# Another order for the first heads of an attention, mixture-of-experts and feed-forward kernel

## The chip, the cores and the metric

The kernel runs on one core of a Trainium2 chip. The metric is the device time of one execution in microseconds. A core has TensorE (PE: matrix products, results to PSUM), VectorE (DVE), ScalarE (ACT), GpSimd (POOL) and SyncE (SP, which here only issues DMA transfers). Each engine works through its own list of instructions in order; a semaphore holds an instruction back until what it needs is there. So the order in which the program is written is the order of each engine's list.

## What is computed

```python
q_bits = (q @ proj) > 0;  k_bits = (k @ proj) > 0        # 6 bits per row: a hash bucket
mask   = q_bucket[:, :, :, None] == k_bucket[:, :, None, :]
scores = where(mask, q @ k.T / sqrt(D), -1e9)            # batch 2, 8 heads, seq 768, D 64
attn   = softmax(scores);  x = attn @ v                  # 16 heads in all
x = moe(x)          # 1536 tokens, width 512: argmax of 8 experts, relu(x w1) w2 times the gate
return moe2(x)      # 512 -> 2048 with a leaky relu -> 512
```

## The kernel before

Attention fills the first 240 us of the execution, and the two feed-forward stages the rest. Products are made in pairs of numbers (a rounded part A and a remainder B), so that the result keeps float32 accuracy.

**One head.** q and k of a head are loaded to a raw tile (`load`), rounded on ScalarE to A, and the remainder B made on GpSimd (`half0`; for head 0 on VectorE). A head's operand tile `op` (`OP[h%5]`, five of them) holds A and B in the places that the products need; the copies are made by ScalarE (`direct`, heads 0 to 2) or by DMA (`OD`, three transfers of A and two of B, for the others all of them). Rows 64 to 75 of two parts of `op` hold the hash bits, one-hot with a large weight: `Z0` (heads 0 and 1) or `Z` makes them in two halves of 384 columns, by three products (`misc<-A,pwh` and so on) and a threshold on VectorE, written into `op` directly by `Z0` and by two more DMA transfers (`op<-big`) by `Z`. Row 96 holds minus the maximum of each query. `clear` zeroes these rows beforehand on GpSimd. `one` and `idle(n)` are n filler products whose result nobody reads.

**The maxima.** Head h has six units u = 6h..6h+5, one for each 128 queries. `MAX(u, a)` makes the masked hash scores against half a of the keys (a product of 384 columns, `mxp`, 0.18 us apart), and VectorE takes the maximum of the half (`mx`). `POSTa` joins the halves (`mt`). For head 0 `mrow(half)` turns three of its columns over (three transposes on TensorE) and VectorE writes the row into `op`. For the others `POSTb` transposes once, VectorE makes `mr`, and one DMA transfer (`op<-mr`) brings it to row 96.

**The scores.** Step s = 6h+j takes 128 keys of head h: `ST(s, 0)` and `ST(s, 1)` are two products each (`st`) and the exponential on ScalarE (`E`), which needs the row of maxima. `EL(s)` makes a float16 rounding `Eh` on ScalarE and the remainder `El` on GpSimd. `AV(s)` multiplies them with the values, 18 products of 64 or 65 columns; it runs four steps behind (`LAG`), for two steps at once at every odd step. v is scaled to float16 first: `vam` (largest absolute value, VectorE, one instruction per head of a group of four), `vscale`, `vscale2` (a chain of six small VectorE instructions to `dg`, and one product), `vsplit` and `vtot`.

**What sets the order.** A loop over steps s writes for each step, in the order of the string `ORDER`, the halves of ST, the halves of MAX, EL, AV, and then what lists tied to the step hold; transfers are collected and issued at `D` of the next step. The table `PLAN` says at which step each of these is written: `Z2`, `Z3` (hash bits of heads 2 and 3), `v0`, `T`, `first` (the router) and others. How far the maxima run ahead is set by `LA` (units below s+6+LA+1 may be written at step s) and, for the first steps, by `cap` (units per step, otherwise two). Two PSUM buffers serve `misc`, five serve `mxp` and `st`. Before the loop the first three steps' first halves are written by hand, among fillers.

Of the kernel before, what the change touches and what calls it, by code (L numbers as in the profile page):

```python
# [11 lines left out]
F16 = mybir.dt.float16  # L12
# [13 lines left out]
LA = 4  # L26
# [14 lines left out]
    v0=(1, 3, 4), T3=(2, 2), Z3=(4, 5), T=(2, 4, 5, 7), Z=(8, 10), ld=0, am1=(4, 6, 8, 9), am=(4, 6, 8,  # L41
    10), sc=(13, 15), tot=3, tot0=6, sp=(-2, 4, 10, 18), cap=(3, 2, 0, 1), x=(1, 2, 7, 3), x3=(0, 1, 2, 2), x4=(9, 10, 13, 11), w1=(91, 92, 95, 96, 97, 98, 99, 100), ga=(87, 88, 90), vl=1, am0=(0, 0), Z2=(0, 1), x6=(0, 1, 6, 4), first=(57, 58, 59, 60, 66, 72, 75, 78, 83, 84, 85, 86),
# [461 lines left out]
def _program(base, tc, nc, q, k, v, proj, mod, w_gate, mbias, w1, w2, win, wout, alpha, out):  # L504
# [203 lines left out]
    clear(1)  # L708
    def half0(h):
        A[h]=ep.tile([128,768],F32R,tag="A",name="A",bufs=2); B[h]=ep.tile([128,768],F32R,tag="B",name="B",bufs=2)  # L710
        nc.scalar.activation(A[h],raw[h],AF.Copy)
        nc.gpsimd.tensor_tensor(out=B[h],in0=raw[h],in1=f32(A[h]),op=ALU.subtract)
    onesh=cp.tile([128,128],F16,tag="onesh",name="onesh")
    VT=cp.tile([33,4,65],F16,tag="vt",name="vt")
    FL=[cp.tile([33,768],F16,tag=f"fl{i}",name=f"fl{i}") for i in range(3)]
# [3 lines left out]
    def fill():  # L719
        for t in DG: nc.gpsimd.memset(t,0.0)  # L720
        nc.gpsimd.memset(onesh,2.0**-8)
        nc.gpsimd.memset(VT[:,:,64:65],0.0)
        nc.gpsimd.memset(VT[0:1,:,64:65],3.0)
        for t in FL: nc.gpsimd.memset(t,0.0)
        for t in VH: nc.gpsimd.memset(t[:,:,:,64:65],1.0)
        clear(3)
        clear(4)
# [87 lines left out]
    def Z0(h,half):  # L815
        p=misc()
        sl=slice(half*384,half*384+384)
        mm(p[0:44,0:384],p0h,A[h][:,sl],start=True,stop=False)
        mm(p[0:44,0:384],p0h,B[h][:,sl],start=False,stop=False)
        mm(p[0:44,0:384],p0l,A[h][:,sl],start=False,stop=True)  # L820
        for o_ in range(2):
            ps=slice(32*o_,32*o_+12)
            nc.vector.tensor_scalar(out=OP[h][64:76,1+o_,sl],in0=p[ps,0:384],scalar1=tv0[ps,0:1],scalar2=tv0[ps,1:2],op0=ALU.is_gt,op1=ALU.mult)
    mx={};flT={}
# [6 lines left out]
    def POSTa(h,c0=0,c1=6):  # L831
        nc.vector.tensor_reduce(out=mts[h%2][:,c0:c1],in_=mx[h][:,c0:c1],axis=AX.X,op=ALU.max)
# [78 lines left out]
    clear(2); half0(2)  # L911
    fill()
    for u in range(3):
        for a in range(2): MAX(u,a)
    POSTa(0,0,3); idle(7); mrow(0)
    for u in range(3,6):
        for a in range(2): MAX(u,a)
    POSTa(0,3,6)
    ahead=(0,1,2)
    Z0(1,0); ST(0,0)  # L920
    idle(2); mrow(1); idle(3); Z0(1,1); ST(1,0)
    for i in range(2): vam(0,slice(i,i+1))
    ST(2,0); idle(5)
    direct(2); OD(1,(3,4)); load(3); OD(2,(1,3,4)); vload(1)
    at(0,lambda:(load(4),load(5))); sl_at(0,flags0)
    for i in range(2): at(PLAN["am0"][i],lambda i=i:vam(0,slice(i+2,i+3)))
# [23 lines left out]
    for s in range(96+LAG+2):  # L950
        us=[u for u in range(nu,min(96,s+6+LA+1,nu+(PLAN["cap"][s] if s<len(PLAN["cap"]) else 2)))]; nu+=len(us)
        fs=dq[:]; dq.clear()
        for o in "aVDNbmnefopAL" if s==0 else ORDER:
# [3 lines left out]
            if o in "ab" and s<96 and not (o=="a" and s in ahead): ST(s,"ab".index(o))  # L957
            if o in "mn":
                for u in us: MAX(u,"mn".index(o))
            if o=="e" and 0<=s-1<96: EL(s-1)  # L960
# [607 lines left out]
```

## Time and profile before

| | |
|---|---|
| median of 3 runs | 687.61 us (685.89 to 688.62) |
| the profiled execution | 686.88 us, of which the span of the trace 685.1 us |
| TensorE busy | 656.4 us (96% of the span), mean granted clock 0.987 |
| VectorE, ScalarE, GpSimd busy | 446.7, 315.3, 236.0 us |

The span is the time from the first to the last instruction. The granted clock is a share of TensorE's full 2.4 GHz: 1.00 or, where it is held back, 0.50 (1.2 GHz); a figure between is a mean over a window. "Idle before" is how long an engine stood still ahead of an instruction, with what released it. Line numbers are those of the kernel before; in the changed kernel the same calls stand one or two lines earlier from `vam` on.

### The profile page before, as it was taken

Reading aid. Unit: us, or ns where it says so; the run is one execution under the profiler, and the core shown is the slowest. Engines: PE = TensorE matmul, PEld = TensorE weight load, DVE = VectorE, ACT = ScalarE, POOL = GpSimd, SP = SyncE. Lnnn points to the kernel's source line nnn. Section 1 sums busy time; section 2 is a strip of 40 time slices with the busy share of each in tenths; the row PEclk is TensorE's granted clock in tenths of the full one; section 3 lists DMA queues with packets and bytes.
Section 4 is the critical chain, followed back from the end, with each engine's and each line's share of the span. In section 5 each row is a group of like instructions: output and inputs, shape, how many; then the busy total and the mean of one; then the engine's idle time right before and its main releaser. Section 6 shows DMA issues by size and latency. Waiting matters only on the chain.

```text
span 685.1 us, 12778 instructions
## 1 busy us (share of the span) xinstructions
PE 656.4 (96%) x4938; PEld 556.2 (81%) x4938; DVE 446.7 (65%) x927; ACT 315.3 (46%) x536; POOL 236.0 (34%) x211
## 2 busy tenths in 40 slices
PE   7789999999999988999999999999999999999995
PEld 6578898998788878898888987888888888888884
DVE  6887878788888778455735668999443444433332
ACT  5567788887787843033423256665211111111111
POOL 8767999987967501310000202040030000200002
PEclk9979999999999999999999999999999999999998
DMA  8466864866603139385320834441020000100001
GB/s 217 129 146 142 187 154 97 185 185 138 140 11 125 49 107 395 119 321 201 108 61 11 285 120 154 131 146 62 1 93 1 15 16 0 47 16 0 1 0 61
DMA packets 32859, 75.02 MB, mean 110 GB/s; under 512 B 7276, under 2 KB 7366, under 8 KB 32534
## 3 DMA queue, kind: packets, MB, share of 16 engines
q1 hardware_dynamic: 29700, 64.43, 33.0%
q0 software_dynamic: 2960, 9.70, 4.3%
q8 instruction: 39, 0.64, 0.4%
q14 instruction: 30, 0.25, 0.1%
q10 hardware_dynamic: 130, 0.00, 0.0%
HBM read 49.79 MB, written 14.68 MB: 94 GB/s over the span
## 4 chain that ended last, share of the span: by engine, by line
PE 54%; DVE 1%; ACT 1%; issue 1%; POOL 1%; ACTq 0%; POOLq 0%
PE o L1413 19%; PE h L1387 18%; PE y L1074 8%; PE g L1054 8%; PE tr L1257 1%; POOL out_dram L1430 1%; PE tr L1041 0%; DVE w L1232 0%; DVE op L1232 0%; ACT op L1230 0%; DVE gl L620 0%; ACT gf L1391 0%; ACT q L1392 0%; ACT w L1230 0%; DVE big L1197 0%
## 5 line engine op out<-in xcount | busy, mean ns | idle before, releaser
L868 POOL TENSOR_TENSOR El<-E,Eh 128x768 f16<-128x768 f32 x87 | 142.7, 1652 | 36.6 <-ACT Eh L867 22.7
L863 ACT ACTIVATE E<-st 128x384 f32<-128x384 f32 x192 | 89.2, 494 | 53.3 <-PE st L862 49.8
L830 DVE TENSOR_REDUCE mx<-mxp 128x1 f32<-128x384 f32 x192 | 97.6, 548 | 9.2 <-PE mxp L829 8.7
L617 ACT ACTIVATE gh<-gf 128x512 fp32r<-128x512 f32 x48 | 30.3, 631 | 142.7 <-PE o L1413 132.2
L867 ACT ACTIVATE Eh<-E 128x768 f16<-128x768 f32 x94 | 79.8, 849 | 0.0
L861 PE MATMUL st<-op 97*128 97x384 f32 x192 | 72.9, 380 | 1.6 <-DMA op<-mr 1.3
L829 PE MATMUL mxp<-op 76*128 76x384 f32 x192 | 65.9, 357 | 7.3 <-ACT E L863 2.5
L620 DVE TENSOR_TENSOR gl<-gf,gh 128x512 fp32r<-128x512 f32 x48 | 33.1, 690 | 59.2 <-ACT gh L617 57.2
L1430 POOL DMA_INDIRECT out_dram<-x,did x12 | 11.8, 984 | 167.8 <-DVE x L1427 89.1
L1387 PE MATMUL h<-big,op 128*128 128x512 f32 x256 | 67.9, 393 | 0.0
L862 PE MATMUL st<-op 128*128 128x384 f32 x192 | 65.8, 343 | 0.0
L1413 PE MATMUL o<-op,gh 128*128 128x512 f32 x192 | 64.2, 395 | 0.0
L1245 POOL DMA_INDIRECT yg<-ys,dpos x10 | 12.3, 1231 | 138.3 <-DVE x L1197 72.8
L876 PE MATMUL av<-vh,Eh 128*128 128x65 f16 x576 | 58.5, 196 | 1.3 <-DVE big L890 1.3
L876 PEld LDWEIGHTS <-Eh 128*128 128x128 f16 x576 | 52.5, 98 | 8.4 <-issue 6.2
L1074 PE MATMUL y<-op,hh 128*128 128x512 f32 x172 | 58.6, 399 | 0.0
L877 PE MATMUL av<-vl,Eh 128*128 128x64 f16 x576 | 58.0, 194 | 0.0
L878 PE MATMUL av<-vh,El 128*128 128x65 f16 x576 | 57.8, 195 | 0.0
L1387 PEld LDWEIGHTS h<-big,op 128*128 128x128 f32 x256 | 48.1, 188 | 10.9
L877 PEld LDWEIGHTS <-Eh 128*128 128x128 f16 x576 | 53.2, 99 | 0.0
L878 PEld LDWEIGHTS <-El 128*128 128x128 f16 x576 | 53.1, 98 | 0.0
L1395 DVE TENSOR_SCALAR gf<-h,al 128x512 f32<-128x512 f32 x33 | 24.8, 751 | 41.7 <-PE h L1387 41.7
(424 smaller groups left out, 1483.2 us busy)
## 6 DMA issues: line engine op xcount, KB each, us to landing
r<-in_moe_w_dram SPq DMA_DIRECT2D x14, 1024.0 KB
op<-B SPq DMA_DIRECT2D x32, 192.0 KB
op<-A SPq DMA_DIRECT2D x28, 192.0 KB
op<-A SPq DMA_DIRECT2D x13, 384.0 KB
ys<-zero SPq DMA_DIRECT2D x19, 256.0 KB
op<-in_moe_w_in_dram SPq DMA_DIRECT2D x4, 1024.0 KB
op<-in_moe_w_out_dram SPq DMA_DIRECT2D x4, 1024.0 KB
ys<-ysb SPq DMA_DIRECT2D x13, 256.0 KB
```

What stands on the lines that cost most here:

```text
L829: mm(p[:,0:384],t[0:76,2,c*128:(c+1)*128],t[0:76,1,a*384:a*384+384],start=True,stop=True)
L830: nc.vector.tensor_reduce(out=mx[h][:,c,a:a+1],in_=p[:,0:384],axis=AX.X,op=ALU.max)
L861: mm(p[:,0:384],t[0:97,1,js],t[0:97,2,qs],start=True,stop=False)
L863: nc.scalar.activation(E[s][0][:,qs],p[:,0:384],AF.Exp,scale=0.125)
L867: else: nc.scalar.activation(eh,e,AF.Copy)
L868: (nc.vector if s>=ELD else nc.gpsimd).tensor_tensor(out=el,in0=e,in1=eh,op=ALU.subtract)
L876: mm(a[:,c*65:c*65+65],eh[:,cs],VH[h//4%2][:,j,h%4,:],start=(j==0 and c==0),stop=False,skip_group_check=True)
L877: mm(a[:,c*65:c*65+64],eh[:,cs],VL[h//4%2][:,j,h%4,:],start=False,stop=False,skip_group_check=True)
L878: mm(a[:,c*65:c*65+65],el[:,cs],VH[h//4%2][:,j,h%4,:],start=False,stop=False,skip_group_check=True)
L1074: nc.tensor.matmul(yps[key][i], a[:, ts], w[:, c], start=(c == 0 and m == 0), stop=(c == 7 and m == 2))
L1387: nc.tensor.matmul(p, terms[t][0][:, kk, cs], terms[t][1][:, kk], start=(n == 0), stop=(n == 11))
L1413: nc.tensor.matmul(po[b][i], a[:, ts], w[:, c % 2], start=(c == 0 and n == 0), stop=(c == 15 and n == 2))
```

## The change

`LA` goes from 4 to 3, and `PLAN` gets other numbers: the maxima of the first steps are spread (`cap`), the hash bits of heads 2 and 3 come at steps 2, 3 and 5, 5, and some of the values' and the router's steps move by one to three. The three tiles `fl` are zeroed by VectorE at the start, not by GpSimd in `fill`; `clear(1)` stands ahead of the small `pw` instructions, `clear(3)` and `clear(4)` around `half0(2)`; `direct(2)` and the transfers behind it stand ahead of the first scores. Head 0's units of maxima are split 4 and 2 around its first `mrow`, not 3 and 3. `Z0(1,0)` gets a callback between its two thresholds. The first halves of steps 0 and 1 and the second half of step 0 are ahead of the loop, with `EL(0)`; ten fillers, not seventeen, stand there. All four `vam(0)` stand ahead of head 1's maxima.

```diff
-LA = 4
+LA = 3
-    v0=(1, 3, 4), T3=(2, 2), Z3=(4, 5), ... tot=3, tot0=6, sp=(-2, 4, 10, 18), cap=(3, 2, 0, 1), ... am0=(0, 0), Z2=(0, 1),
+    v0=(1, 2, 4), T3=(2, 2), Z3=(5, 5), ... tot=2, tot0=6, sp=(-1, 5, 11, 17), cap=(2, 2, 1, 1, 0, 0, 1), ... Z2=(2, 3),
...
+    FL=[cp.tile([33,768],F16,tag=f"fl{i}",name=f"fl{i}") for i in range(3)]
+    for t in FL: nc.vector.memset(t,0.0)
...
     clear(0)
+    clear(1)
...
-        for t in FL: nc.gpsimd.memset(t,0.0)
-        clear(3)
-        clear(4)
...
-    def Z0(h,half):
+    def Z0(h,half,mid=None):
...
+            if o_==0 and mid: mid()
...
-    clear(2); half0(2)
-    fill()
+    clear(2); fill(); clear(3)
+    half0(2); direct(2); OD(1,(3,4)); load(3); OD(2,(1,3,4)); vload(1)
+    clear(4)
     for u in range(3):
         for a in range(2): MAX(u,a)
-    POSTa(0,0,3); idle(7); mrow(0)
-    for u in range(3,6):
+    POSTa(0,0,3)
+    MAX(3,0); MAX(3,1); idle(5); mrow(0)
+    for u in range(4,6):
         for a in range(2): MAX(u,a)
     POSTa(0,3,6)
-    ahead=(0,1,2)
-    Z0(1,0); ST(0,0)
-    idle(2); mrow(1); idle(3); Z0(1,1); ST(1,0)
-    for i in range(2): vam(0,slice(i,i+1))
-    ST(2,0); idle(5)
-    direct(2); OD(1,(3,4)); load(3); OD(2,(1,3,4)); vload(1)
+    ahead=((0,0),(0,1),(1,0))
+    def mid():
+        ST(0,0); ST(1,0); idle(1); mrow(1)
+    Z0(1,0,mid)
+    ST(0,1); EL(0); idle(2); Z0(1,1); idle(2)
+    for i in range(4): vam(0,slice(i,i+1))
     at(0,lambda:(load(4),load(5))); sl_at(0,flags0)
-    for i in range(2): at(PLAN["am0"][i],lambda i=i:vam(0,slice(i+2,i+3)))
...
-            if o in "ab" and s<96 and not (o=="a" and s in ahead): ST(s,"ab".index(o))
+            if o in "ab" and s<96 and (s,"ab".index(o)) not in ahead: ST(s,"ab".index(o))
-            if o=="e" and 0<=s-1<96: EL(s-1)
+            if o=="e" and 0<s-1<96: EL(s-1)
```

VectorE's list before, from the second joined maxima of head 0 (`mt`) to the first small instruction of `vscale` (`op1` is head 1's operand tile, `mx_370` its maxima, `am` the values' largest magnitudes):

```order
L832 TENSOR_REDUCE mt0_181<-mx_249 128x3
L823 TENSOR_SCALAR op1_140<-misc_301,tv0_128 12x384 x2
L846 TENSOR_SCALAR op0_139<-misc_317 1x384
L823 TENSOR_SCALAR op1_140<-misc_326,tv0_128 12x384 x2
L731 TENSOR_REDUCE am_339<-vr_117 128x1 x2
L830 TENSOR_REDUCE mx_370<-mxp_371 128x1
...
L731 TENSOR_REDUCE am_339<-vr_117 128x1 x2
L851 TENSOR_SCALAR ft_397<-misc_395 6x128
L809 TENSOR_SCALAR big2_74<-misc_399,tv_127 24x384
...
L736 TENSOR_REDUCE misc_429<-misc_429 4x1
```

And VectorE's list now, from the same place to the same place:

```order
L831 TENSOR_REDUCE mt0_189<-mx_260 128x3
L821 TENSOR_SCALAR op1_140<-misc_310,tv0_128 12x384
L845 TENSOR_SCALAR op0_139<-misc_331 1x384
L821 TENSOR_SCALAR op1_140<-misc_310,tv0_128 12x384
L821 TENSOR_SCALAR op1_140<-misc_346,tv0_128 12x384 x2
L729 TENSOR_REDUCE am_355<-vr_117 128x1 x4
L829 TENSOR_REDUCE mx_360<-mxp_361 128x1
...
L850 TENSOR_SCALAR ft_379<-misc_377 6x128
...
L734 TENSOR_REDUCE misc_399<-misc_399 4x1
```

The second row of maxima moved between the two thresholds of head 1's first half; all four `am` stand ahead of head 1's reductions; ten reductions and two hash thresholds (L809) stood ahead of the small chain, and now eight reductions and no hash threshold.

SyncE's list before, where head 2's row of maxima is sent (`op2<-mr`), with the copies for head 5 (`op0<-A`, `op0<-B`) and the hash rows of heads 4 and 5 (`op4<-big2`, `op0<-big2`):

```order
L838 DMA op2_141<-mr_729 1x6x128
L842 DMA fl2_189<-ft_732 1x6x128 x2
L650 DMA op0_139<-A_702 64x2x768
L650 DMA op0_139<-A_702 64x768 x2
L650 DMA op0_139<-B_703 64x768 x2
L650 DMA op4_143<-big2_74 12x768 x2
L650 DMA op0_139<-big2_74 12x768 x2
```

And SyncE's list now, at the same place:

```order
L650 DMA op0_139<-A_676 64x2x768
L650 DMA op0_139<-A_676 64x768 x2
L650 DMA op0_139<-B_677 64x768 x2
L837 DMA op2_141<-mr_822 1x6x128
L650 DMA op4_143<-big2_74 12x768 x2
L650 DMA op0_139<-big2_74 12x768 x2
L841 DMA fl2_155<-ft_825 1x6x128 x2
```

Head 2's row was sent ahead of the five copies for head 5, and is now sent behind them. No later head changes its place against the copies in this way.

## Rows read from the trace of the kernel before

**Rows 1.** Windows of 20 us: length, busy time (count) per engine, TensorE clock, DMA share, GB/s.
```profile
20.00:40.00 20.00, 15.80 (x70) 11.51 (x69) 17.53 (x43) 11.76 (x19) 13.53 (x10) 0.81 0.51 137
340.00:360.00 20.00, 20.00 (x88) 16.19 (x87) 6.55 (x9) 3.83 (x5) 0.00 (x0) 1.00 0.24 78
```

**Rows 2.** TensorE in order of time: start, length, instruction, idle before and releaser.
```profile
31.98 0.40 PE L747 MATMUL misc<-dg,one 128*128 128x4 f32 x2 [1.54 <-DVE dg L743]
...
40.82 0.28 PE L876 MATMUL av<-vh,Eh 128*128 128x65 f16 x1
...
42.65 0.34 PE L802 MATMUL misc<-A,pwh 128*24 128x384 f32 x1
...
43.18 0.34 PE L861 MATMUL st<-op 97*128 97x384 f32 x1
...
51.44 0.36 PE L882 MATMUL av<-vt,fl 33*128 33x65 f16 x6
...
57.08 0.42 PE L861 MATMUL st<-op 97*128 97x384 f32 x1
```

**Rows 3.** VectorE in order of time, the same columns.
```profile
4.51 0.51 DVE L695 TENSOR_SCALAR p0h<-pj 64x6 fp32r<-64x6 f32 x4 [1.81 <-DMA pj<-in_proj_dram]
...
15.34 0.55 DVE L846 TENSOR_SCALAR op<-misc 1x384 fp32r<-1x384 f32 x1 [1.55 <-PE misc L845]
...
19.03 1.36 DVE L823 TENSOR_SCALAR op<-misc,tv 12x384 fp32r<-12x384 f32 x2
...
22.59 1.01 DVE L731 TENSOR_REDUCE am<-vr 128x1 f32<-128x384 f32 x2
...
23.64 2.88 DVE L830 TENSOR_REDUCE mx<-mxp 128x1 f32<-128x384 f32 x6
...
31.71 0.21 DVE L743 TENSOR_SCALAR dg<-misc,a 4x4 f32<-4x4 f32 x1
...
37.38 0.56 DVE L760 TENSOR_TENSOR vl<-misc,vh 128x384 f16<-128x384 f32 x1
```

**Rows 4.** A window of 4 us, columns as in the first group.
```profile
32.00:36.00 4.00, 3.34 (x11) 2.70 (x12) 2.25 (x7) 1.80 (x5) 3.24 (x2) 0.53 0.66 134
```

**Rows 5.** ScalarE in order of time.
```profile
22.32 1.48 ACT L794 ACTIVATE op<-big 64x1536 fp32r<-64x1536 f32 x1
```

**Rows 6.** GpSimd in order of time.
```profile
17.09 2.08 POOL L724 MEMSET fl<- 33x768 f16 x3
```

**Rows 7.** SyncE, which issues the transfers, in order of time.
```profile
45.78 2.85 SPq L650 DMA_DIRECT2D op<-A  x3
...
48.74 1.75 SPq L650 DMA_DIRECT2D op<-B  x2
...
51.89 0.77 SPq L838 DMA_DIRECT2D op<-mr  x1
...
80.61 0.76 SPq L838 DMA_DIRECT2D op<-mr  x1
...
118.62 0.71 SPq L838 DMA_DIRECT2D op<-mr  x1
```

**Rows 8.** TensorE around the rows of maxima of heads 4 and 9.
```profile
85.85 0.45 PE L861 MATMUL st<-op 97*128 97x384 f32 x1 [0.71 <-DMA op<-mr]
...
116.65 0.27 PE L835 MATMUL misc<-ident,mt 128*6 128x128 f32 x1
...
120.00 0.42 PE L861 MATMUL st<-op 97*128 97x384 f32 x1
...
123.72 0.42 PE L861 MATMUL st<-op 97*128 97x384 f32 x1
```

**Rows 9.** A window of 0.2 us behind the transfer issued at 118.62 us.
```profile
119.80:120.00 0.20, 0.20 (x4) 0.20 (x3) 0.00 (x0) 0.20 (x1) 0.20 (x1) 1.00 0.04 10
```

**Rows 10.** Who waited for whom, TensorE, 40 to 80 us.
```profile
PE mxp L829 <- DMA op<-big: 1.3, 1, 1.3
```

**Rows 11.** The same from 80 to 120 us.
```profile
PE st L861 <- DMA op<-mr: 0.7, 1, 0.7
```

More of the change, by code (lines that the diff above doesn't have):

```diff
@@ L40 @@
 PLAN = dict(
-    v0=(1, 3, 4), T3=(2, 2), Z3=(4, 5), T=(2, 4, 5, 7), Z=(8, 10), ld=0, am1=(4, 6, 8, 9), am=(4, 6, 8,
-    10), sc=(13, 15), tot=3, tot0=6, sp=(-2, 4, 10, 18), cap=(3, 2, 0, 1), x=(1, 2, 7, 3), x3=(0, 1, 2, 2), x4=(9, 10, 13, 11), w1=(91, 92, 95, 96, 97, 98, 99, 100), ga=(87, 88, 90), vl=1, am0=(0, 0), Z2=(0, 1), x6=(0, 1, 6, 4), first=(57, 58, 59, 60, 66, 72, 75, 78, 83, 84, 85, 86),
+    v0=(1, 2, 4), T3=(2, 2), Z3=(5, 5), T=(2, 4, 5, 7), Z=(8, 10), ld=0, am1=(5, 6, 8, 9), am=(4, 6, 8,
+    10), sc=(13, 15), tot=2, tot0=6, sp=(-1, 5, 11, 17), cap=(2, 2, 1, 1, 0, 0, 1), x=(1, 2, 7, 3), x3=(0, 1, 2, 2), x4=(9, 10, 13, 11), w1=(91, 92, 95, 96, 97, 98, 99, 100), ga=(87, 88, 90), vl=1, Z2=(2, 3), x6=(0, 1, 6, 4), first=(57, 58, 59, 60, 66, 72, 78, 80, 81, 84, 85, 86),
 )
@@ L707, in _program @@
     mts=[cp.tile([128,6],F32,tag=f"mt{i}",name=f"mt{i}") for i in range(2)]
-    clear(1)
     def half0(h):
@@ L714, in _program @@
     VT=cp.tile([33,4,65],F16,tag="vt",name="vt")
-    FL=[cp.tile([33,768],F16,tag=f"fl{i}",name=f"fl{i}") for i in range(3)]
     VH=[cp.tile([128,6,4,65],F16,tag=f"vh{i}",name=f"vh{i}") for i in range(2)]
```

## The prediction

> **What bounds the kernel now.** I read the windows first. In the second feed-forward stage TensorE is busy in every microsecond (20.00 of 20.00 us at full clock), with VectorE at 6.55 us; between 20 and 40 us it has 15.80 of 20.00 us at a mean clock of 0.81, while VectorE has 17.53 [rows 1]. So the end is set by TensorE's list, and a microsecond that the beginning loses is not given back later; but in the beginning itself TensorE waits for VectorE. Then the order in time. TensorE stands 1.54 us for the value scale `dg` at 31.98 [rows 2], and from there its clock is down: the window at 32 us has 0.53, which is mostly the 1.2 GHz level [rows 4]. The first product with the values starts at 40.82 and its pair of steps ends at 42.65, the first score of head 1 is at 43.18, the fourth pair of steps' end (row `vt,fl`) at 51.44, the first score of head 2 at 57.08 [rows 2]. VectorE's rows say why so late: its list from 15.34 on has one idle stretch of 1.55 us, for head 0's first row of maxima, and then runs to `dg` (ends 31.92); `vl`, without which no product with the values starts, ends at 37.94 [rows 3]. The last views are the waits behind it: 1.3 us of TensorE for hash rows that come by DMA [rows 10], 0.7 us for a row of maxima [rows 11].
>
> Unit prices from these rows: a reduction 2.88/6 = 0.48 us, a magnitude `am` 0.50, a threshold 1.36/2 = 0.68 [rows 3]; products of 384 columns follow each other every (43.18 - 42.65)/3 = 0.18 us at full clock [rows 2].
>
> **The change, step by step.**
>
> *Head 0's rows of maxima.* VectorE now has two reductions (0.96 us) to do in the 1.55 us in which it waited. Ten filler products instead of fourteen (each `idle` is two) stand behind two products more, so the first row comes about 0.1 later; four reductions are left behind it and not six. The joined maxima, ready for 19.03 before, come at about 18.15: 0.85 earlier.
>
> *Head 1's hash bits.* First threshold 18.2 to 18.9, second `mrow` (its transposes run meanwhile) to 19.45, other threshold to 20.1. Then TensorE has ST(0,1), which waited for that row, four filler products and the three hash products, about 1.5 us; VectorE waits 0.9 us, and the last two thresholds end at 22.35. Before, `am` followed them at 22.59 [rows 3]. So 0.6 of the 0.85 is lost again. Four `am` follow, not two: 2.0 us. Head 1's first reduction starts at 24.3, and stood at 23.64 [rows 3]: 0.65 later.
>
> *To the scale.* Before, VectorE spent 31.92 - 23.64 = 8.3 us from there to the end of `dg` [rows 3]. Of that two reductions (0.96), two thresholds (1.3) and two `am` (1.0) are no longer in between: about 5.2 us are left, and `dg` ends near 29.6, 2.3 us earlier. Then `vl`: four reductions, two thresholds, the copies of scale and joined maxima, and the pair `vh`, `vl` are 1.9 + 1.3 + 0.3 + 1.1 = 4.6 us: 34.3, where it was 37.94. TensorE has the scores of steps 4 and 5 by then (they wait for ScalarE's E alone), so the pair of steps takes its 42.65 - 40.82 = 1.83 us [rows 2] and ends at 36.15: 6.5 us earlier. But it leaves behind what had been done before it: eight products of maxima (two steps' worth, units 12 to 15) and the three of head 3's first hash half, 11 x 0.18 = 1.95 us. Net 4.55 us.
>
> *Steps 6 to 9.* The units that `cap` put off come here, and VectorE has for these four steps two thresholds, fourteen reductions, three `am`, two vt copies and a pair `vh`, `vl`: 1.3 + 6.8 + 1.5 + 0.45 + 1.1 = 11.1 us, where TensorE has about 8.1. From 36.9, where the first hash product behind the pair is done, that is 48.0; TensorE's last product of step 9 stands ahead of some 1.1 us of it, so 46.9. Before it was 51.44 + 0.36 = 51.8 [rows 2]; one unit (0.35 us) is still owed. Net 4.55: kept.
>
> *Head 2's row of maxima.* It is written at step 10 and not 8, behind the five copies for head 5. From step 9's end to head 2's first score TensorE needs 57.08 - 51.8 = 5.3 us [rows 2], so it is ready at 52.2. SyncE, from head 1's row at 35.9: row 0.75, flags 1.45, a load 1.2, hash rows 1.6, five copies 2.85 + 1.75 [rows 7], a load 1.2, five copies as long but for waits: some 15 us, so head 2's row is issued at 50.9. Uncongested, data of such a row move 1.2 us after the issue (118.62, then 119.80 [rows 7, 9]); behind copies it took 85.85 - 80.61 = 5.2 us, by head 4's wait that ended there [rows 7, 8]. Bounds of the stall: 0 and 3.9 us. About 2.5 us from issue to use, between the two and nearer the first because SyncE's own issuing has spread the copies: 53.4, a stall of 1.2 us. Net 3.4.
>
> *The 1.3 us wait for hash rows* [rows 10] is that of head 4's first maxima. `LA` = 3 writes these maxima a step later, and their rows are not sent later than before against the steps. It goes: +1.3. Net 4.7.
>
> *The clock.* TensorE will stand some 1.7 us at 23 to 24.8, behind the four `am`, with five buffers full of products. What it did before the row at 31.98 was a gap of 1.54, and the clock went to half [rows 2, 4]. I expect the same here. At half clock the scores of steps 2 to 5 are hidden behind VectorE, but the pair of steps and the hash products behind it may be up to 1.4 us slower: I take half, -0.7. Net 4.0.
> The Trainium skill (TensorE: Matmul & The Clock Gate, Why this matters for your kernels) asks for a clearly longer gap than this before the clock falls in mid-kernel; the granted clock of 0.53 behind a gap of 1.54 [rows 2, 4] speaks against that. By the page this term would be 0 and the sum 4.7.
>
> *At no cost.* The zeroing of `fl`: 2.08 us on GpSimd [rows 6]; on VectorE it lies in the 1.81 us for which VectorE waits for `proj` [rows 3]; if it takes as long there, 0.27 us come on the path, if it is quicker nothing: I take 0. GpSimd's other clearings change places, and of 20 to 40 us it was busy for 13.53 [rows 1]: no cost, at worst the 0.27 of above once more. `direct(2)`, 1.48 us and a second copy, stood among the first exponentials [rows 5], and now ahead of them where ScalarE has nothing to do: 0 to 0.5 gained, taken as 0. The router's and values' steps moved by one to three: nothing in the trace prices them; such waits are of 0.3 to 1.3 us [rows 10, 11], so -1.3 to 1.3, taken as 0.
>
> *`LA` for the later heads.* Their rows of maxima are made one step later, each behind a product pair with the values. For head 9 the transpose at 116.65 would stand at 120.00, with the first score at 123.72 [rows 8]: 3.7 us are left. Needed are 118.62 - 116.65 = 2.0 us to the issue, less if VectorE is free by then, and 1.2 to 1.6 to the landing: 3.2 to 3.6. It just fits: 0. For the other half of the heads SyncE is the last, as at 80.61, whose transfer waits for copies and not for the maxima: 0.
>
> Sum: the profiled execution's 686.88 - 4.0 = 682.9; the median of the runs lies 0.7 above that execution, so 683.6 us.
>
> **The rivals.**
> *The start's gain is swallowed.* The clock stays at 1.2 GHz through steps 6 to 9, or head 2's row takes the full 5.2 us: the sum is then 4.7 - 1.4 - 2.7 or so, 0.6 us of gain, and 2.4 with half of either: 685.2 to 687.0, in the middle 686.1. For it: both costs have their rows [rows 4, 11]. Against: TensorE is steadily fed from step 4 on, and the copies are issued over 15 us.
> *Everything falls well.* No half clock, head 2's row in time, a copy or two more hidden: 4.7 + 1.1 and up to 1 more, near 681.3. Against: each is a bound.
> *Slower: the rows of maxima of the later heads.* `LA` = 3 leaves 3.7 us from transpose to use [rows 8]. It decides from the point where transpose, VectorE's queue, issue and landing take more than that. With 2.0 to the issue and a landing a third of the way from 1.6 to head 4's 5.2, 2.8, each of the seven heads that are placed as head 9 waits 2.0 + 2.8 - 3.7 = 1.1 us, and perhaps the other seven too: 7 x 1.1 = 7.7, or 15, less 4: 691 to 699. For it: head 4's row came 0.7 late already [rows 8, 11]. Against: the pair of products in front of the later transpose gives VectorE time to be free, so the first term shrinks.
> *It does not do what it says:* head 1's reductions start later, not earlier, and if `vl` waits for ScalarE and not for VectorE, the first product with the values stays near 40: 687.6 plus the 0.35 owed, less 1.3: about 686.7.
>
> **Chances.** Forecast (gain 2.4 to 5.5) 0.50, swallowed 0.20, everything well 0.14, slower 0.11, not what it says 0.05. From no change a measurement of this kernel can tell 0.5%, 3.4 us: the forecast's case lies above that with about 0.36 of its 0.50, and with the third 0.50 are faster; 0.11 slower; 0.39 within. The range holds 8 in 10 if it runs from 681.0 (gain 6.6) to 688.4: it leaves out the slower case and the end of the good one. The forecast's own range is 682.1 to 685.2.
>
> **What would show it.** Right: `dg` near 29.6 and `vl` near 34.3, the pair of steps ending near 36, no 1.3 us wait of TensorE for `op<-big` in 40 to 80 us; a wait for `op<-mr` of about 1 us near 53. Wrong: waits of TensorE for `op<-mr` at many heads after 100 us (slower); a clock of 0.5 beyond 40 us (swallowed); `vl` later than 36. If TensorE's idle time after 100 us differs by more than 1.5 us from before, the steps that I took as 0 were not.

## The result, and the profile after

| | median us (executions) | ratio to before, 95% interval |
|---|---|---|
| before | 687.4 (4) | |
| changed | 697.2 (4) | 1.0142 [1.0105, 1.018] |

The changed kernel is slower: 9.8 us, where a gain of 4 was forecast and the range ended at 688.4. The profiled execution took 699.72 us, its span 697.9 us; TensorE was busy for 661.3 us of it at a mean clock of 0.979.

The windows of the changed kernel, columns as in [rows 1]:

```profile
20.00:40.00 20.00, 15.15 (x90) 10.75 (x88) 14.13 (x35) 9.61 (x17) 10.76 (x8) 0.74 0.62 155
60.00:80.00 20.00, 19.78 (x255) 17.61 (x255) 14.46 (x41) 15.34 (x29) 15.85 (x13) 0.89 0.38 86
80.00:100.00 20.00, 17.61 (x231) 16.11 (x229) 11.96 (x31) 12.94 (x24) 14.46 (x16) 0.91 0.62 143
340.00:360.00 20.00, 20.00 (x88) 16.20 (x87) 12.49 (x15) 8.31 (x11) 0.00 (x0) 1.00 0.27 93
```

The feed-forward stage is as full as in [rows 1], so what the attention loses is not given back. In the attention TensorE is now idle for 2.4 us of the window from 80, and its clock is below 1.00 in windows after 60 us, where before it never was.

TensorE in order of time, answering to [rows 2, 8]:

```profile
24.21 0.69 PE L828 MATMUL mxp<-op 76*128 76x384 f32 x1 [2.36 <-DVE mx L829]
...
30.47 0.42 PE L745 MATMUL misc<-dg,one 128*128 128x4 f32 x2
...
35.84 0.20 PE L875 MATMUL av<-vh,Eh 128*128 128x65 f16 x1 [0.28 <-DVE vh L757]
...
37.47 0.33 PE L800 MATMUL misc<-A,pwh 128*24 128x384 f32 x1
...
39.95 0.45 PE L860 MATMUL st<-op 97*128 97x384 f32 x1 [1.26 <-DMA op<-mr]
...
49.64 0.35 PE L881 MATMUL av<-vt,fl 33*128 33x65 f16 x6
...
57.98 0.66 PE L860 MATMUL st<-op 97*128 97x384 f32 x1 [2.43 <-DMA op<-mr]
...
90.55 0.44 PE L860 MATMUL st<-op 97*128 97x384 f32 x1 [2.39 <-DMA op<-mr]
```

And VectorE's, answering to [rows 3]:

```profile
23.60 1.95 DVE L829 TENSOR_REDUCE mx<-mxp 128x1 f32<-128x384 f32 x4
...
28.66 0.21 DVE L741 TENSOR_SCALAR dg<-misc,a 4x4 f32<-4x4 f32 x1
...
35.82 0.56 DVE L758 TENSOR_TENSOR vl<-misc,vh 128x384 f16<-128x384 f32 x1
...
39.82 1.25 DVE L807 TENSOR_SCALAR big<-misc,tv 24x384 f32<-24x384 f32 x2 [2.60 <-DMA op<-big]
```

The beginning is faster, as forecast: the first pair of steps ends at 37.47 and not at 42.65, the first score of head 1 is at 39.95 and not at 43.18. But the first score of head 2 is at 57.98, where it was 57.08, behind a wait of 2.43 us for its row of maxima, and head 4's is at 90.55, where it was 85.85, behind one of 2.39. The waits of TensorE, 36 to 240 us (total, times, longest), before and then changed, against the 0.7 us of [rows 11]:

```profile
PE mxp L829 <- DMA op<-big: 1.3, 1, 1.3
...
PE st L861 <- DMA op<-mr: 1.3, 2, 0.7
```

```profile
PE st L860 <- DMA op<-mr: 10.0, 6, 2.4
```

The wait for hash rows is gone, as forecast; the wait for rows of maxima has grown from 1.3 to 10.0 us. The six are at heads 1, 2, 4, 6, 8 and 10; behind head 1 no odd head waits. At heads 4 to 10 they are 2.39, 1.24, 1.80 and 0.86 us, 6.3 in all.

They cost more than their length. The changed kernel behind the wait that ended at 90.55, in half microseconds:

```profile
91.00:91.50 0.50, 0.50 (x4) 0.50 (x4) 0.11 (x1) 0.23 (x1) 0.00 (x0) 1.00 0.38 61
91.50:92.00 0.50, 0.50 (x4) 0.50 (x3) 0.45 (x1) 0.49 (x2) 0.00 (x0) 0.54 1.29 168
...
94.50:95.00 0.50, 0.50 (x14) 0.50 (x12) 0.06 (x1) 0.41 (x1) 0.42 (x2) 0.54 0.04 12
95.00:95.50 0.50, 0.50 (x21) 0.50 (x19) 0.00 (x0) 0.00 (x0) 0.42 (x2) 1.00 0.00 0
```

From about 91.5 to 95.0 the clock is at 1.2 GHz, and TensorE, busy all the time, does half the work: 1.7 us are lost. The same stretch stands behind heads 8 and 10 (none behind head 6's wait of 1.24), and one twice as long, 57.4 to 64.2, which begins within head 2's wait.

So the sum closes. Between the first scores of heads 3 and 11 the changed kernel falls 11.0 us behind before (from 2.9 to 13.95 us). Waits: 6.3, less the 1.25 that heads 4 and 10 waited before, 5.0. Half clock: three times 1.7, 5.1. That is 10.1 of 11.0 us. (These are single executions, whose spans, 697.9 and 685.1 us, are 12.8 us apart; the medians differ by 9.8.)

**Why the even heads' rows are late.** SyncE of the changed kernel, and then the same place of before:

```profile
62.78 0.43 SPq L76 DMA_DIRECT2D mi<-in_moe_modality_id_dram  x1
70.10 0.76 SPq L837 DMA_DIRECT2D op<-mr  x1
...
73.03 2.80 SPq L650 DMA_DIRECT2D op<-A  x3
...
78.87 2.70 SPq L650 DMA_DIRECT2D op<-A  x3
...
84.75 0.75 SPq L837 DMA_DIRECT2D op<-mr  x1
```

```profile
64.80 0.59 SPq L72 DMA_DIRECT2D mb<-n_moe_modality_bias_dram  x1
65.50 0.77 SPq L838 DMA_DIRECT2D op<-mr  x1
...
68.94 2.83 SPq L650 DMA_DIRECT2D op<-A  x3
```

The rows at 70.10 and 65.50 are head 3's, that at 84.75 is head 4's. Before, SyncE came to head 3's row at 65.4 and the row was there. Now it stands from 63.2 to 70.1, because that row is made a step later, and ten copies, four loads and the row of head 4 stand behind it. From 70.10 to 84.75 it issues without a pause. Against the first score of head 3 (70.49 before, 73.40 now) the first copy starts 1.55 us ahead before and 0.37 ahead now. Head 4's row is issued 11.35 us behind that score (10.12 before), is used 5.8 us after its issue (5.2 before), and so is late by 2.39 us (0.71 before).

### The profile page after: what moved, and what is told of

The parts are those of the page before. It is cut to its first block, busy times and chain, and to the rows that moved or that the text cites. A ratio compares the mean times of both kernels' runs of the same rounds, so it can differ in the third digit from the quotient of the medians.

```text
span 697.9 us, 12749 instructions
## 1 busy us (share of the span) xinstructions
PE 661.3 (95%) x4924; PEld 559.5 (80%) x4924; DVE 448.2 (64%) x930; ACT 316.3 (45%) x536; POOL 234.4 (34%) x208
## 4 chain that ended last, share of the span: by engine, by line
PE 53%; DVE 1%; ACT 1%; issue 1%; POOL 1%; ACTq 0%; POOLq 0%
PE o L1413 18%; PE h L1387 17%; PE y L1074 8%; PE g L1054 8%; PE tr L1257 1%; POOL out_dram L1430 1%; PE tr L1041 0%; DVE w L1232 0%; DVE op L1232 0%; ACT op L1230 0%; DVE gl L620 0%; ACT gf L1391 0%; ACT q L1392 0%; ACT w L1230 0%; DVE big L1197 0%
## 5 line engine op out<-in xcount | busy, mean ns | idle before, releaser
L862 ACT ACTIVATE E<-st 128x384 f32<-128x384 f32 x192 | 89.6, 492 | 64.2 <-PE st L861 63.6
L860 PE MATMUL st<-op 97*128 97x384 f32 x192 | 74.9, 390 | 11.3 <-DMA op<-mr 10.0
L828 PE MATMUL mxp<-op 76*128 76x384 f32 x192 | 68.3, 367 | 6.1 <-DVE mx L829 2.9
L861 PE MATMUL st<-op 128*128 128x384 f32 x192 | 67.5, 352 | 0.0
L1413 PE MATMUL o<-op,gh 128*128 128x512 f32 x192 | 64.2, 395 | 0.0
L875 PE MATMUL av<-vh,Eh 128*128 128x65 f16 x576 | 60.8, 199 | 1.3 <-DVE big L889 1.0
L875 PEld LDWEIGHTS <-Eh 128*128 128x128 f16 x576 | 53.8, 100 | 8.9 <-issue 5.9
L876 PE MATMUL av<-vl,Eh 128*128 128x64 f16 x576 | 60.0, 196 | 0.4 <-DVE vl L758 0.4
L877 PE MATMUL av<-vh,El 128*128 128x65 f16 x576 | 59.8, 197 | 0.0
L876 PEld LDWEIGHTS <-Eh 128*128 128x128 f16 x576 | 54.4, 101 | 0.0
L860 PEld LDWEIGHTS st<-op 97*128 97x128 f32 x192 | 37.9, 197 | 17.9 <-DMA op<-mr 8.3
```

Of the source, the lines that this page charges most:

```text
L828: mm(p[:,0:384],t[0:76,2,c*128:(c+1)*128],t[0:76,1,a*384:a*384+384],start=True,stop=True)
L860: mm(p[:,0:384],t[0:97,1,js],t[0:97,2,qs],start=True,stop=False)
L862: nc.scalar.activation(E[s][0][:,qs],p[:,0:384],AF.Exp,scale=0.125)
L875: mm(a[:,c*65:c*65+65],eh[:,cs],VH[h//4%2][:,j,h%4,:],start=(j==0 and c==0),stop=False,skip_group_check=True)
L876: mm(a[:,c*65:c*65+64],eh[:,cs],VL[h//4%2][:,j,h%4,:],start=False,stop=False,skip_group_check=True)
L877: mm(a[:,c*65:c*65+65],el[:,cs],VH[h//4%2][:,j,h%4,:],start=False,stop=False,skip_group_check=True)
```

## The experiments

Eighteen kernels ran. One table holds them, by how far the first score of a head stands behind before's in the profiled execution. These columns are of single executions: the first score of head 0 stood between 15.3 and 18.1 us among kernels whose beginnings are alike up to there, so only differences inside a row are read, "lost 3 to 11" above all. The kernel before ran again beside each group of runs, with medians of 685.0 to 687.4 us, so two kernels are better compared by their ratios than by their medians.

| kernel | LA | median us | ratio to before, interval | head 1 | head 2 | head 3 | lost 3 to 11 |
|---|---|---|---|---|---|---|---|
| changed | 3 | 697.2 | 1.0142 [1.0105, 1.018] | -3.2 | 0.9 | 2.9 | 11.0 |
| e1 LA = 4 | 4 | 685.95 | 1.0005 [0.9986, 1.0024] | -3.0 | 1.1 | 0.1 | 2.2 |
| e2 before, LA = 3 | 3 | 696.34 | 1.0163 [1.0123, 1.0203] | -1.8 | -2.3 | -1.6 | 8.65 |
| e3 copies later | 3 | 701.09 | 1.0238 [1.0197, 1.0278] | -2.5 | 0.2 | 1.2 | 9.8 |
| e4 the same | 4 | 693.9 | 1.0135 [1.0093, 1.0177] | -1.9 | 1.65 | 1.7 | 3.4 |
| e5 odd rows early | 3 | 698.07 | 1.0191 [1.0159, 1.0224] | -3.7 | 3.0 | 5.1 | 5.4 |
| e6 even rows early | 3 | 696.78 | 1.0156 [1.0101, 1.0211] | -2.1 | -0.5 | -0.2 | 9.0 |
| e7 rows by ScalarE | 3 | 696.12 | 1.0154 [1.0126, 1.0183] | -2.0 | 3.7 | 5.65 | 3.6 |
| e8 the same | 4 | 688.19 | 1.004 [1.0024, 1.0057] | -2.4 | 2.4 | 4.8 | -0.2 |
| e9 constant odd rows | 3 | 693.83 | 1.0128 [1.0103, 1.0153] | -1.9 | 3.3 | 5.3 | 3.4 |
| e10 all constant | 3 | 691.36 | 1.0082 [1.0064, 1.0101] | -1.5 | 3.5 | 5.1 | 0.75 |
| e11 head 2 early | 4 | 693.14 | 1.0115 [1.0097, 1.0133] | 1.3 | 5.25 | 8.1 | -0.6 |
| e12 fillers | 3 | 699.39 | 1.0196 [1.0175, 1.0218] | -1.6 | 2.9 | 4.9 | 10.7 |
| e13 fewer fillers | 3 | 696.46 | 1.0157 [1.0122, 1.0193] | -3.1 | 1.6 | 2.3 | 7.7 |
| e14 units made up | 4 | 690.73 | 1.0055 [1.0031, 1.0078] | -2.6 | 1.7 | 7.3 | -0.6 |
| e15 fillers at 23 us | 4 | 686.87 | 1.0015 [0.9996, 1.0034] | -3.1 | 1.1 | 1.6 | 0.1 |
| e16 both | 4 | 689.28 | 1.0055 [1.0036, 1.0074] | -3.2 | 2.4 | 3.8 | 0.1 |
| e17 LA = 5 | 5 | 695.34 | 1.0134 [1.0099, 1.0168] | -2.0 | 2.3 | 1.7 | 5.9 |
| e18 before, LA = 5 | 5 | 702.12 | 1.0262 [1.0225, 1.03] | -0.5 | 2.2 | 3.2 | 7.8 |

All are edits of the changed kernel, but e2 and e18, which are edits of before.

### Is it `LA`? (e1, e2)

```diff
-LA = 3
+LA = 4        # e1; in e2, in the kernel before: 4 -> 3
```

> The changed kernel with LA = 4, as before; the rest of the change stays. Theory A (the row of maxima of every second head is made a step later and its transfer then lies behind the five copies' data): from head 4 on the kernel is as before, with waits for op<-mr of 0.7 us at head 4 and 0.5 at head 10 and no clock drops behind them; what stays is the loss up to head 3, whose first score stood 2.9 us later than before, so about 690. Rival B (the loss comes from the new beginning and the moved PLAN entries, not from LA): no change, about 697.

> The kernel before with LA = 3 alone. Theory A: heads 4, 6, 8 and 10 wait 0.9 to 2.4 us each and TensorE drops to half clock behind three of these waits; between the first scores of heads 3 and 11 the changed kernel lost 11 us so, and this one loses about as much: 696 to 699. Rival B: about 687.5, the same as before.

Yes, from both sides: with `LA` = 4 the changed kernel is the kernel before in time, and the kernel before with `LA` = 3 is as slow as the changed one. Rival B falls. e1 comes out 4 us under its expectation: head 2's wait is 1.6 us here, the clock doesn't drop behind it, and of the 2.9 us at head 3 only 0.1 is there. But it has one drop that was not expected, from 87.9 to 91.3 us behind head 4's wait of 0.91; most of the 2.2 us that it loses from head 3 to 11 lie there. e2 has one drop and not three, from 85.3 to 92.1 around head 4's wait of 1.97, and none behind head 8's of 1.72. The waits (e1, then e2):

```profile
PE st L860 <- DMA op<-mr: 4.0, 4, 1.6
```

```profile
PE st L861 <- DMA op<-mr: 5.0, 4, 2.0
```

### Rows ahead of the copies (e3, e4)

```diff
-T=(2, 4, 5, 7)
+T=(2, 4, 5, 9)        # e3; e4: LA = 4 and T=(2, 4, 5, 8)
```

> The changed kernel with LA = 3, but T=(2,4,5,9) for (2,4,5,7): the five copies of every odd head are issued two steps later, behind the row of maxima of the even head before it, head 2's too. Theory A: all waits of 0.9 us and more for op<-mr from head 2 on go, and with them the clock drops; head 1's stays (1.3 us). The start's 3.2 us at head 1 are kept: 684 to 685. Rival C (the row is a step later on TensorE and VectorE, and the copies matter little): the even heads wait still, about 1 us each or more, and the time stays above 692.

> The changed kernel with LA = 4 and T=(2,4,5,8): rows a step earlier again and ahead of the copies. Theory A: like the run with rows first and LA = 3, or up to 0.5 us better: 683.5 to 685, no wait for op<-mr over 0.5 us behind head 1. Rival C: the same, since LA is undone. Rival B: about 695.

Both missed, and on the slow side: the copies could not be put off for nothing. In e3 no even head waits for its row behind head 2, but head 3 does, and the first maxima of heads 6, 8 and 10 wait 1.70, 1.97 and 1.84 us. e3, and then e4:

```profile
PE mxp L828 <- ACT E L862: 6.0, 6, 2.0
PE st L860 <- DMA op<-mr: 4.0, 3, 1.6
PE mxp L828 <- DMA op<-big: 1.7, 1, 1.7
```

```profile
PE mxp L828 <- DMA op<-big: 3.8, 3, 1.4
```

The three waits of e3 look like one kind, though the view names two releasers:

```profile
93.34 0.41 PE L828 MATMUL mxp<-op 76*128 76x384 f32 x1 [1.70 <-DMA op<-big]
...
121.57 0.41 PE L828 MATMUL mxp<-op 76*128 76x384 f32 x1 [1.97 <-ACT E L862]
...
152.36 0.41 PE L828 MATMUL mxp<-op 76*128 76x384 f32 x1 [1.84 <-ACT E L862]
```

The exponential named at 152.36 ends at 152.37, too late to have released it, and SyncE began to issue these heads' hash rows 3.4, 3.6 and 3.5 us ahead (89.91, 117.99, 148.85). So hash rows (`op<-big`) are the likelier cause of all three, 5.5 us, as they are named in e4. They stand behind the copies in SyncE's list too. What was taken from the rows was paid by the hash rows. So the question became whose lateness it is.

### Whose row holds the queue? (e5, e6, e9, e10)

```diff
-sl_at(s+PB,lambda h=u//6:POSTb(h))
+sl_at(s+(0 if u//6%2 else 1),lambda h=u//6:POSTb(h))     # e5: odd heads a step earlier
+sl_at(s+u//6%2,lambda h=u//6:POSTb(h))                   # e6: even heads a step earlier
```

> The changed kernel with LA = 3, but the rows of maxima of the odd heads alone are made one step earlier (in the step of the last unit, not behind the next step's pair of products); even heads as changed. Theory D: SyncE issues in order and stands idle ahead of an odd head's row (63.2 to 70.1 us in the changed kernel), with ten copies, four loads and the next even head's row queued behind it; from the odd row's issue to the even row's it then needs 14.7 to 15.6 us of issuing, so the odd row's lateness is the even row's. Odd rows 3 to 4 us earlier take the even heads' waits (0.9 to 2.4 us) and the clock drops behind them away, though these rows are not touched; new are waits of TensorE for VectorE's joined maxima at 7 heads, 0 to 1 us each: 686 to 692. Rival C (each row is late by its own step): the even heads' waits stay, 697 or more.

> The mirror of the run with early odd rows: the rows of the even heads alone one step earlier. Theory D: an even head's row is ready on VectorE sooner, but its transfer's place in SyncE's list is reached at the same time as in the changed kernel (the issue is set by the odd row in front): the waits for op<-mr at heads 4, 6, 8 and 10 stay within 0.5 us each, 696 to 700. Rival C: these waits go, 686 to 692.

By the waits theory D holds. In e5, where no even row was touched, heads 4 to 10 wait not at all for `op<-mr`; in e6, where the even rows are made earlier, they wait 2.21, 0.57, 1.32 and 1.54 us, 5.6 in all beside 6.3 (two of them differ by 0.7 from the changed kernel's, where at most 0.5 was expected). By the time e5 missed: the early transposes now wait for VectorE's joined maxima, up to 2.2 us a time, not 0 to 1. e5, and then e6:

```profile
PE misc L834 <- DVE mt L831: 10.0, 7, 2.2
...
PE st L860 <- DMA op<-mr: 1.2, 2, 1.0
```

```profile
PE st L860 <- DMA op<-mr: 6.9, 5, 2.2
PE misc L834 <- DVE mt L831: 1.7, 4, 0.9
```

A row must therefore go without a new wait: a constant tile `mz`, sent behind the head's own copies. These two kernels leave out the heads' own maxima (the odd heads' in e9, those of all heads from 3 on in e10), so only their waits are of use.

```diff
+        if h>2 and h%2: later(lambda: ... OP[h][96:97,2] <- mz ...,1)    # e9, in OD; e10: if h>2
-        nc.sync.dma_start(... <- mr)
+        if not(h>2 and h%2): nc.sync.dma_start(... <- mr)
```

> The changed kernel with LA = 3. Leaves out: the rows of maxima of the odd heads from 3 on; a constant row is sent in their place, right behind the copies of the same head, so that SyncE waits for no odd row. Even heads keep their own rows. Theory D (SyncE held by the odd row holds the copies, loads and even row behind it): waits for op<-mr of heads 4, 6, 8 and 10 fall from 6.3 us in all to under 2, the three drops to half clock behind them (3.4 us each, 1.7 us lost each) go, and of the 11.0 us that the changed kernel loses against before between the first scores of heads 3 and 11 at most 3 stay: 687 to 691. If the even rows wait for data in the DMA engines whatever stands in front, the waits stay at 1 us and more and the time over 694.

> As the run with constant odd rows, and the even heads from 4 on as well: no row of maxima of heads 3 to 15 is waited for (leaves out those rows). If the rows are the whole price of LA = 3, the loss between the first scores of heads 3 and 11 falls to 1 us or less: 686 to 688. If LA = 3 also costs through VectorE's and ScalarE's timing (joined maxima and exponentials later against TensorE), the time stays over 690.

e9 touches only odd rows, and the even heads' waits fall to 0.99, 0.60, 1.03 and 0.51 us, 3.1 where under 2 was expected; no clock drop is left after 70 us, and the loss from head 3 to 11 falls from 11.0 to 3.4. So most of it was SyncE held by the odd rows. In e10 0.75 us is left: the rows are nearly the whole price of `LA` = 3 from head 3 on (the kernel before itself waits 1.25 us for rows there, so up to 2.0 us may have other causes). Neither gets the expected time, since both are over 2 us later at head 3 than the changed kernel: head 2's row is waited for 3.5 and 3.3 us (2.4 there). One added transfer stands ahead of that row in the list; but e12 and e13, without it, waited 2.8 and 3.0 us, so how much is its doing stays open.

### Another queue (e7, e8)

```diff
-nc.sync.dma_start(out=f32(OP[h%NP][96:97,2, ...
+nc.scalar.dma_start(out=f32(OP[h%NP][96:97,2, ...      # e7; e8: with LA = 4
```

> The changed kernel with LA = 3, the rows' transfers (op<-mr) issued by ScalarE and not by SyncE; nothing else. Theory D: SyncE is never held by a row, the copies go out earlier, and the row doesn't stand behind them in the list: no waits over 0.5 us for op<-mr from head 4 on; ScalarE pays the issue and now and then waits for the row: 684 to 689. Rival E (the row is delayed by the copies' data in the DMA engines, whichever queue it is in): issued some 1 to 2 us earlier but landing 4 us and more after the issue, so heads 2, 4 and 8 wait 1 us still: 690 to 695.

> LA = 4 with the changed beginning, and the rows issued by ScalarE. Theory D: the waits for op<-mr that LA = 4 left (0.7 at head 1, 1.6 at head 2, 0.9 at head 4, 0.8 at head 10) fall below 0.5 each, 4.0 us in all to 1: 683 to 685 beside 686 with SyncE. Rival E: within 1 us of the run with LA = 4.

Mixed, and both times lie above what either theory expected. From head 3 to 11 e7 does what D says: 3.6 us lost, and 0.16 and 0.58 us of wait at heads 6 and 8. At head 2 it does what E says. ScalarE and then TensorE in e7, and the same two in e8:

```profile
55.79 0.69 ACTq L837 DMA_DIRECT2D op<-mr  x1
56.58 0.49 ACT L862 ACTIVATE E<-st 128x384 f32<-128x384 f32 x1 [2.04 <-DVE mx L829]
```

```profile
60.82 0.66 PE L860 MATMUL st<-op 97*128 97x384 f32 x1 [4.02 <-DMA op<-mr]
```

```profile
56.39 0.69 ACTq L837 DMA_DIRECT2D op<-mr  x1
...
59.45 0.66 PE L860 MATMUL st<-op 97*128 97x384 f32 x1 [2.62 <-DVE vl L758]
```

In e7 head 2's row was issued as soon as it was made (55.49 + 0.27), from another engine than the copies, and was used 5.0 us later all the same. In e8 the view counts only 0.8 us of waits for rows, but it puts the 2.62 us ahead of head 2's first score down to `vl`, which no score reads and which ended just then (59.33). At this place e7 waits for the row, and here the row was issued 3.1 us before; so it is the likelier releaser, the waits for rows in e8 are 3.4 us beside 4.0 in e1, and nothing was won. So a row pays twice: for its place in the issuing list, and, as the 5.0 us suggest, for the data ahead of it. The Trainium skill (DMA: Bandwidth & Descriptors, Issuing engines are not separate DMA queues) says that transfers of all issuing engines run on the same engines and interleave; the 5.0 us agree. It adds that a second issuer saves only issue time, usually small beside the transfer. Here it also frees SyncE from standing for the rows (63.2 to 70.1 us in the changed kernel), and from head 3 to 11 e7 loses 3.6 us where the changed kernel loses 11.0.

### The clock's share (e12, e13, e15)

```diff
+            if o=="a" and s in (24,48,60):       # e12: 16, 12, 5 products; e13: (24,48), 8 and 6
+                p=misc()
+                for _ in range(...): mm(p[:,0:128],one,one,start=True,stop=True)
```

> The changed kernel, and 16, 12 and 5 filler products (0.13 us each at full clock, 2.0, 1.5 and 0.6 us) ahead of the first scores of heads 4, 8 and 10, where TensorE waits 2.4, 1.8 and 0.9 us for the row of maxima. The rows come as late as before. If the drops to half clock behind these waits come from TensorE standing still: they go, 3 x 1.7 us: 692 to 693. If they come from something else (the work that follows): no change, 697, or up to 1 more where the fillers last longer than the wait.

> The changed kernel with LA = 3, and 8 and 6 filler products ahead of the first scores of heads 4 and 8 (0.24 us each by the first filler run, where 16 took 3.8 us: 1.9 and 1.4 us), where TensorE waited 2.4 and 1.8 us for the row. If the half clock behind these two waits (3.4 us each) comes from standing still: the clock stays at 1.00 at both, and between the first scores of heads 3 and 11 the loss falls from 11.0 by 2 x 1.7 to about 7.6 us; time 693 to 694.5. If the waits alone were the loss: no change, 697.

By its time e12 decided nothing: a filler takes 0.24 us and not 0.13, so 16 of them lasted 3.8 us where the wait was 2.4. But from 66.3 us to the end of the attention its clock stays at 1.00. e13 has fewer fillers. TensorE and its windows in e13 at head 4:

```profile
87.74 2.02 PE L959 MATMUL misc<-one 128*128 128x128 f32 x16 [0.15 <-DVE vl L758]
89.78 0.44 PE L860 MATMUL st<-op 97*128 97x384 f32 x1
```

```profile
89.50:91.50 2.00, 1.98 (x13) 1.79 (x12) 0.88 (x2) 1.00 (x3) 0.00 (x0) 1.00 0.69 94
91.50:93.50 2.00, 2.00 (x53) 1.84 (x51) 1.26 (x3) 2.00 (x4) 1.23 (x1) 1.00 0.70 286
93.50:95.50 2.00, 2.00 (x17) 1.99 (x13) 1.62 (x6) 1.52 (x4) 1.84 (x3) 1.00 0.13 52
```

The row is issued as late as ever (84.00 us), but the clock stays at 2.4 GHz. From head 4 to 5 this kernel loses nothing against before, where the changed one lost 1.5 us, and from 8 to 9 it loses 0.6 for 2.1. From 3 to 11 it is 7.7, as expected. (One drop came new, at 118.5 us behind head 6's wait of 1.12 us, and that behind head 10 did not come.) The median of 696.46 is above what was expected and can't be told from 697.2: that the half clock costs 1.7 us a time is read from these stretches, not from the total. Nor does every such wait bring the drop. TensorE in e6 at head 4, without fillers:

```profile
87.42 0.45 PE L860 MATMUL st<-op 97*128 97x384 f32 x1 [2.21 <-DMA op<-mr]
```

```profile
88.00:90.00 2.00, 2.00 (x22) 1.84 (x21) 1.74 (x4) 1.87 (x4) 0.09 (x1) 1.00 0.71 153
```

The clock stays at 1.00 there, and so it does in e5 behind waits of 1.94 and 2.24 us (124.3 and 182.2 us). So a full clock at one head could be chance; that it stayed full at four places with fillers (heads 4 and 8 in e12 and in e13) makes that less likely.

e15 puts eight idle products for two ahead of head 1's maxima, with `LA` = 4.

```diff
-    ST(0,1); EL(0); idle(2); Z0(1,1); idle(2)
+    ST(0,1); EL(0); idle(2); Z0(1,1); idle(8)
```

> LA = 4 with the changed beginning, and eight idle products for two behind head 1's second hash half, so that TensorE stands still 1 us and not 2.4 ahead of head 1's maxima, where VectorE makes the four largest magnitudes. If that gap is what drops the clock (0.50 from 26 to 36 us in the run with LA = 4): it stays at 1.00 or drops later, first score of head 1 is up to 3 us earlier than 40.2, and the time 683 to 685. Rival: VectorE and ScalarE set these steps and TensorE's half speed is hidden behind them: head 1 within 0.7 us, time 686.

The time is the rival's, and head 1 is where it was. But the edit did not keep the clock up: it drops 1.5 us later, from 27.9 to 34.7 us (26.4 to 36.7 in e1), over the products that lead to `vl`. So whether the half speed of the beginning is hidden stays open.

### Can the beginning's gain be kept? (e11, e14, e16)

```diff
-cap=(2, 2, 1, 1, 0, 0, 1)
+cap=(2, 2, 1, 1, 0, 1)        # e11; e14 and e16: (2, 2, 1, 1, 0, 0); all with LA = 4, e16 with e15's idle(8)
```

> LA = 4 with the changed beginning, and cap = (2,2,1,1,0,1) for (2,2,1,1,0,0,1): head 2's last unit of maxima a step earlier, so that its row is issued ahead of the five copies for head 5. With LA = 4 alone head 2 waited 1.6 us for its row. If that wait goes and VectorE has room for two reductions more by step 5: 1 to 2 us under that run's 686, so 684 to 685, 2 us better than before. Rival: VectorE is full there, the reductions push the values' scale or head 2's maxima later: 686 or more.

> LA = 4 with the changed beginning, cap = (2,2,1,1,0,0) without the last 1: the units of maxima put off in steps 4 and 5 are made up from step 6 on, head 2's last one a step earlier, its row ahead of the copies for head 5, and nothing more for VectorE before the values' scale. If head 2's row is what takes the beginning's gain back: its wait of 1.6 us goes, first score of head 2 at 56.5, time 684 to 685. Rival: VectorE is full in steps 6 to 9 and makes the row no earlier: within 0.7 us of 686.

> Both edits. If both work, 682 to 684, and better than the kernel before by more than 0.3%. If only one works, as that one; if the row of head 2 is VectorE's matter and the clock is hidden, 686.

No, all three missed. Head 2's row goes out ahead of the copies for head 5 and is in time, and then its neighbour in the queue is late. e14:

```profile
PE mxp L828 <- DMA op<-big: 2.5, 1, 2.5
```

These are head 4's hash rows at 66 us. SyncE stood for head 2's row until 55.5 us, with the copies for head 5 and these hash rows behind it in the list: it is the mechanism of the later heads once more. e11 waits 2.6 us there, and 4.5 us for head 2's hash rows at 39.7 besides, since head 2's first maxima now stand ahead of head 1's first score; so it loses the beginning too (head 1 at 44.49).

### More lead (e17, e18)

```diff
-LA = 3
+LA = 5        # e17; in e18, in the kernel before: 4 -> 5
```

> The changed kernel with LA = 5. If the rows alone set the price: waits for op<-mr behind head 2 (with LA = 4: 0.9 at head 4, 0.8 at head 10) go, 684 to 685.5. Rival: maxima a step earlier need their hash rows a step earlier, and these lie behind the copies: waits for op<-big of 1 us and more at even heads, where LA = 4 has none, with half clock behind some: 688 to 695.

> The kernel before with LA = 5. If the rows alone set the price: the waits of 0.7 (head 4) and 0.5 (head 10) go: 684.5 to 686. Rival: its wait of 1.3 us for hash rows at 63 us grows by about a step's worth and others come: 688 to 695.

The rival holds by its waits; its range of 688 to 695 is passed by 0.3 us in e17 and by 7 in e18, and that excess stays open. Rows are early behind head 2, and the hash rows, which the maxima read, are late. e18 has no wait for `op<-mr`, and these:

```profile
PE mxp L829 <- DMA op<-big: 7.3, 6, 1.8
```

`LA` = 4 is the place between: one step less and the rows are late, one step more and the hash rows are. No version beat the kernel before; e1 equals it.

## Why the prediction was wrong

**The step that failed** is the second half of the term on `LA`: "For the other half of the heads SyncE is the last, as at 80.61, whose transfer waits for copies and not for the maxima: 0." It took the copies as a fixed point. They are not: the odd head's row in front of them is made from the maxima, and SyncE waits for it in order. A step of lateness there moves the ten copies and the even row with them (70.10, 73.03, 84.75), and the even row had no slack: it was 0.71 us late already [rows 8]. The runs showed 11.0 us lost between heads 3 and 11 in its place: all but 2.2 of them go with `LA` = 4 (e1), 8.65 come with `LA` = 3 alone (e2), all but 3.4 go when SyncE waits for no odd row (e9), and all but 0.75 when it waits for no row behind head 2's (e10).

**The first half of that term** was right: the odd heads, 3.2 to 3.6 us needed of 3.7, wait nowhere behind head 1 (heads 3 and 9 need 0.6 us and not 2.0 from transpose to issue).

**The slower rival** happened, with 691 to 699 foretold and 697.2 measured, but at other heads than it priced: it had the heads placed as head 9 wait, which don't, and the even ones as "perhaps the other seven too". So that its range holds the measured time is luck. It counted no half clock, which is about half of the loss. What was held against it, "gives VectorE time to be free", looked at the wrong engine: SyncE's list was the one to follow from row to row.

**The beginning.** Against the forecast: `dg` ended at 28.87 (29.6), `vl` at 36.38 (34.3), the pair of steps at 37.47 (36.15), 5.2 us earlier than before where 6.5 was said. `vl` was 2 us late since products at half clock fed VectorE (0.32 us apart) and ScalarE's part came last (0.69 us of wait). Steps 6 to 9, "Net 4.55: kept.", failed: the end of step 9 was at 50.0 and not 46.9. The pair of steps was 1.3 late, and head 1's first score stood 2.5 us behind its end where it had stood 0.5 before: three more hash products are ahead of it, and 1.26 us of waiting for head 1's row, for which no term stood. From there it took 10.0 us, with TensorE standing only 0.3. VectorE stood 2.60 us at 39.82, because the moved hash steps of head 3 write a tile from which head 2's hash rows were still being sent; no term had this either, but TensorE did not wait for it. Head 2's row was then made at 54.5, not 52.2, and the stall was 2.43 and not 1.2. The half clock from 57.4 to 64.2 took about 3.1 more (half of the 6.3 us in which TensorE worked); the loss grows by only 2.0 from head 2 to head 3, since the wait of 1.3 us for hash rows went there. e1 says what the beginning is worth by itself: nothing, since 3 us at head 1 are gone at head 2. Whether the order of SyncE's list or the bytes around head 2 bound it is not settled: in e11 and e14 the wait only changes its name, but e14's SyncE stood for a row ahead of it; a version with fewer bytes there was not tried.

**Right:** the 1.3 us wait for hash rows went; the clock fell (at 23.3) in the gap that ended at 24.21. The Trainium skill (TensorE: Matmul & The Clock Gate, HAM oscillation — how this bites in real kernels) allows longer gaps than these in mid-kernel; the drops behind 2.39 us at head 4 and 1.80 at head 8, and e13's clock of 1.00 where the gap was filled, speak against it, as [rows 2, 4] did. The 2.21 us in e6 without a drop agree with it.

## What to carry to other kernels

A transfer that waits in an in-order list is a wait for all that is queued behind it: cost a later producer at the last consumer of that list, not at its own. Where one resource serves two streams with deadlines (here rows and hash rows), a lead has a best place, and shortening it shows first where the slack is already negative in the trace. A wait of TensorE of about 2 us in mid-kernel may bring half clock behind it, which in the changed kernel cost about as much again (5.1 us beside 5.0); it doesn't come each time, so it belongs in a range.

## What the runs showed of the hardware

- In the changed kernel the clock fell to 1.2 GHz for 3.4 us behind stands of 2.39, 1.80 and (with smaller ones ahead of it) 0.86 us, each time about 1 to 2 us after TensorE had started again; behind 1.24 us it did not. In other runs it fell behind 1.12 us (e13) and 0.91 us (e1), and stayed at 1.00 behind 2.21 us (e6), 1.94 and 2.24 us (e5). The length of the stand alone doesn't tell.
- A transfer of 3 KB was used 3.4 to 5.8 us after its issue where even heads of the changed kernel waited for it, and 5.0 us after it when ScalarE issued it (e7); where nothing else moved, its data moved 1.2 us after the issue [rows 7, 9].
